# Output projection's weights in eight-row runs per partition, with the attention output reordered on the chip to match

## The chip, the cores and the metric

The kernel runs on one core of one Trainium2 chip. The metric is the device time of one execution in microseconds (us). Three runs of the kernel before gave 369.44, 369.52 and 369.91 us, a median of 369.52 us. The profile was taken on one further execution of 369.39 us.

## The reference, cut to what matters

One decode step of a gated mix of two branches. Branch A is attention over the last 2048 positions of a cache (8 batches, 32 query heads on 16 key/value heads of width 128), followed by an output projection with `wo` (4096 x 576). Branch B is a layer norm and a two-layer network of width 4608 with biases `b1` and `b2`. A gate per batch mixes them.

```python
g = sigmoid((A_x * gate_w).sum(-1, keepdims=True))
q = (A_x @ wq)                                   # 8 x 32 heads x 128
p = softmax(q . k[last 2048] * 128 ** -0.5)
a = (p @ v[last 2048]).reshape(8, 1, 4096) @ wo  # 4096 x 576
b = gelu(layernorm(B_x) @ w1 + b1) @ w2 + b2     # 576 -> 4608 -> 576
out = g * a + (1 - g) * b                        # 8 x 1 x 576
```

Nearly all of the data is the cache: 32 units of keys and 32 of values, each of 2 MB.

## The kernel before

**The plan.** The kernel isn't written in the order in which it runs. Every piece of work is an `_Op` with an engine, a cost estimate, dependencies (`deps`, for which the engine waits) and order-only predecessors (`after`). `_Plan.schedule` plays the program through with those estimates and so fixes the list of each engine; `emit` then writes the lists out, each op with its waits on the semaphores of its `deps`. At run time each engine goes through its own list from the top, so an op that waits holds everything behind it in that list. Where an op stands in the list is thus decided by estimated times and not by the real ones. For transfers the estimate has two forms, and the size that is passed to `dma(...)` chooses between them:

```python
if op.nbytes < 65536:
    op.t1 = est + 0.4 + self.DMA_LAT            # DMA_LAT = 1.8
else:
    start = max(est + 0.4, dma_free)            # behind all earlier large transfers
    dma_free = start + op.nbytes / self.DMA_BW
    op.t1 = dma_free + self.DMA_LAT
```

**The transfers.** All large loads are issued by SP, in the order of the list `stream` (from L540): five units of keys (K0 to K4), then a K unit and a V unit in turn, a chunk of `wo` (W0 to W3) after every eighth V unit, then the bias `b2` ("B") and four chunks of `w2` (M0 to M3). Its end reads ... V23, W2, K29, V24, K30, V25, K31, V26, V27, V28, V29, V30, V31, W3, B, M0, M1, M2, M3. The loads go round nine slots of 2 MB in SBUF; each waits until its slot is free. By that rule W3 waits for the transposes of K30, M0 for the value matmuls of V25, M1 for the transposes of K31, M2 for the value matmuls of V26 and M3 for those of V27; V31 waits for those of V24, V30 for the transposes of K29 and V29 for the projection with W2. `b2` has a place of its own and waits for nothing but its turn in SP's list.

**Keys** (`k_unit`, L612 on). A K unit is one of four quarters of a group of two key heads; there are eight groups. DVE transposes its two halves (L630, "tr"), with two buffers for the results, and PE multiplies each half with the queries (L644, "qk", eight matmuls a half). After the fourth quarter comes the softmax of the group (`softmax`, L574 on): maximum on DVE (L577), small steps (L580 to L586), four exponentials on ACT (L591), four transposes on DVE (L596), the sum over the positions (L599, L600, one PE matmul at L601, a reciprocal at L602), and at L606 `rg`, the reciprocal times the gate.

**Values** (`v_unit`, L656 on). PE multiplies the probabilities with a V unit (L667, "pv", sixteen matmuls), ACT copies the result out of PSUM (L673, "ovac"), PE sums and transposes it (L678, "osel"). After two V units, one "item" (a key head with two query heads and all eight batches) is complete: ACT copies it (L689, "oev"), and POOL multiplies it with `rg` into `oT` (L697). The last item, 15, does without ACT and POOL: there DVE reads PSUM directly. `oT` holds, for each of the 32 heads, the 128 head columns on the partitions and the eight batches beside each other.

**Projection and second layer.** `wo_chunk` (L701 on) loads eight heads' rows of `wo`, so that partition p gets row p of each head: eight runs of 1152 bytes a partition. `AccGroup` (L523 to L536) adds products into one PSUM bank: for each pair (left operand, right operand) two matmuls of 288 columns (L532), one per half of the 576 output columns. Four such groups belong to a W chunk, one per item. `bias` (L716 on) loads `b2` onto eight partitions in one transfer (L717) and adds it in with a group "m2_b" of four matmuls; `m2_chunk` (L721 on, transfers at L728) does the same for `w2`, the last chunk in three pieces. At the end DVE and ACT copy half of the bank each (L746, L747), and two transfers write the output (L749).

**PE's list around the end of the value stream**, before the change: qk of K30, pv of V25, osel of V25, qk of K31, pv of V26, osel of V26, pv of V27, the sum of the last group (L601), osel of V27, then pv and osel of V28 to V31 in turn, and last 92 matmuls of L532: 16 for the four items of W3, 4 of "m2_b", 72 of `w2`.

Of the kernel before, what the change touches and what calls it, by code (L numbers as in the profile page):

```python
# [171 lines left out]
def build_kernel(nc, A_x, A_k_cache, A_v_cache, A_wq, A_wo, B_x, B_w1, B_b1, B_w2, B_b2, gate_w, out):  # L172
# [24 lines left out]
    with ExitStack() as es:  # L197
# [39 lines left out]
        req("sm", 32 * NG, F32)  # L237
        req("dsum", 32, F32)
        req("rr", 32, F32)
        req("rg", 2 * 32, F32)  # L240
        req("o32", 2 * 16, F32)
        req("oT", Hkv * 16, BF)
        req("out_sb", JN, BF)
        req("PT", 2 * 2048, BF)
        req("P", 2048, BF)
# [57 lines left out]
        rg = view("rg").rearrange("p (g m) -> p g m", g=2)  # L303
        o32 = view("o32").rearrange("p (u m) -> p u m", u=2)
        oT = view("oT").rearrange("p (u h b) -> p u h b", u=Hkv, h=2)
# [20 lines left out]
        def col(i, parts=128):  # L326
# [9 lines left out]
        BK_ACC = 7  # L336

        eng_sems = {e: es.enter_context(nc.semaphore("sem_" + e)) for e in ENGS}
        dma_keys = ["x", "b", "b2", "wq", "w1", "out", "outb"] + ["s%d" % i for i in range(NSLOT)] + ["t%d" % i for i in range(4)]
        dma_sems = {k: es.enter_context(nc.semaphore("dma_" + k)) for k in dma_keys}  # L340

        P = _Plan()
# [5 lines left out]
        o_ident = add("pool", lambda e: e.affine_select(out=ident, in_=ones_bf[:, 0:128], pattern=[[-1, 128]], compare_op=ALU.is_equal,  # L348
                                                        fill=0.0, base=0, channel_multiplier=1), deps=[o_ones], name="ident", cost=0.3)
        o_idf = add("pool", lambda e: e.tensor_copy(idf8, ident[0:8, 0:8]), deps=[o_ident], name="idf8", cost=0.15)  # L350
        o_nhalf = add("pool", lambda e: e.memset(col(C_NHALF, 8), -0.5), name="nhalf", cost=0.1)
        o_xz0 = add("pool", lambda e: e.memset(view("xz", 8), 0.0), name="xz0", cost=0.2)
        o_yz0 = add("pool", lambda e: e.memset(view("yz", 8), 0.0), name="yz0", cost=0.2)
# [207 lines left out]
        o_ev, o_sel = {}, {}  # L561
        proj_ops = {}
        oT_done = {}

        def src_of(cache, g, q):
            hkv, b0 = 2 * g + q // 2, 4 * (q % 2)
# [7 lines left out]
        def softmax(g):  # L574
            k = lambda i, n=1, parts=128, p0=0: sm[p0:p0 + parts, g, i:i + n]
            MX, GA, GB_, GC_, M01, M23, TT, NB, SUM, S = 0, 1, 2, 3, 4, 5, 6, 7, 8, 12
            mx = add("dve", lambda e: e.tensor_reduce(out=k(MX), in_=ps[:, 0:4, :].rearrange("p a n -> p (a n)"), axis=AXL.X, op=ALU.max), deps=[qk_unit[4 * g + 3]], name="mx%d" % g, cost=2.25, prio=5)  # L577
# [22 lines left out]
            ds = add("dve", lambda e: e.tensor_scalar(out=dsum, in0=i32, scalar1=k(S), scalar2=None, op0=ALU.mult), deps=[s_] + o_i32 + ([rg_done[g - 1]] if g else []), name="ds_%d" % g, cost=0.16, prio=5)  # L600
            sp_ = add("pe", lambda e: e.matmul(ps[:, BK_S, 0:32], ones_f, dsum, start=True, stop=True), deps=[ds, o_yT, o_gb], name="sum_pe%d" % g, cost=0.5, prio=5)  # L601
            rc = add("dve", lambda e: e.reciprocal(out=rr, in_=ps[:, BK_S, 0:32]), deps=[sp_], name="rc_%d" % g, cost=0.16, prio=5)  # L602

            def rg_fn(e):
                in1 = bass.AP(arena_f, offset=foffs("gb"), ap=[[AST // 2, 128], [0, 2], [1, 8], [0, 2]])
# [4 lines left out]
            rg_done[g] = add("dve", rg_fn, deps=deps, name="rg_%d" % g, cost=0.16, prio=5)  # L610

        def k_unit(i):  # L612
            g, q = divmod(i, 4)
# [42 lines left out]
        def v_unit(i):  # L656
# [28 lines left out]
            if q % 2 == 1:  # L685
                hl = q // 2
                o_acc = ps[:, BK_OS[0]:BK_OS[1] + 1, 0:8]
                if item < Hkv - 1:
                    ev = add("act", lambda e: e.activation(out=o32[:, item % 2, :].rearrange("p (a n) -> p a n", a=2), in_=o_acc, func=ACTF.Copy), deps=[o_sel[i - 1], o_sel[i]] + ([oT_done[item - 2]] if item >= 2 else []), name="oev%d" % item, cost=0.25, prio=3)  # L689
                    o_item_ev[item] = ev  # L690
                    eng, src_, deps = "pool", o32[:, item % 2, :], [ev, rg_done[g]]
                else:
                    eng, src_, deps = "dve", o_acc, [o_sel[i - 1], o_sel[i], rg_done[g]]

                def om_fn(e):
                    src4 = src_.rearrange("p a (b h) -> p a b h", h=2) if item == Hkv - 1 else src_.rearrange("p (a b h) -> p a b h", a=2, h=2)
                    return e.tensor_tensor(out=oT[:, item, :, :].rearrange("p h (a b) -> p a b h", a=2), in0=src4,  # L697
                                           in1=rg[:, g % 2, 16 * hl:16 * hl + 16].rearrange("p (a b h) -> p a b h", a=2, h=2), op=ALU.mult)
                oT_done[item] = add(eng, om_fn, deps=deps, name="oT%d" % item, cost=0.25, prio=9)

        def wo_chunk(i):  # L701
            s = take_slot()
            h0 = WO_CH * i
            dst = slot(s)[:, 0:WO_CH * WOP].rearrange("p (t c) -> p t c", t=WO_CH)
            d = dma("sp", lambda e: e.dma_start(dst[:, :, 0:D], A_wo[128 * h0:128 * (h0 + WO_CH), :].rearrange("(t p) c -> p t c", p=128)),
                    "s%d" % s, WO_CH * 128 * D * 2, deps=slot_free[s], name="d_wo%d" % i, after=last_dma[-1:])
            last_dma.append(d)
            ops = []
# [3 lines left out]
            slot_free[s] = ops  # L712

        o_m2 = []

        def bias(i):  # L716
            d = dma("sp", lambda e: e.dma_start(b2_sb, B_b2.partition_broadcast(8)), "b2", 65536, name="d_b2", after=last_dma[-1:])  # L717
            last_dma.append(d)
# [101 lines left out]
```

## Time and profile before

| what | value |
|---|---|
| profiled execution, device time | 369.39 us |
| its span, first to last instruction | 367.7 us |
| around the span | 1.7 us |
| PE busy | 260.6 us (71%) |
| DVE busy | 210.0 us (57%) |
| ACT busy | 47.7 us (13%) |
| POOL busy | 37.5 us (10%) |
| read from HBM | 154.31 MB, 420 GB/s over the span |
| mean granted TensorE clock | 0.838 |

"Busy" is the share of the span in which an engine works on an instruction; a wait isn't busy. The start of the span is time 0 in everything that follows. A row of the timeline gives start, duration, engine, line of the kernel, operation, operands, shape and number of instructions merged into the row, and in brackets how long the engine had been idle before it and what ended that. "SPq" rows are the issuing of a transfer by SP, not the transfer; the rows on issues give the time from issue to landing. The rows of DMA packets count packets "under 512 B", "under 2 KB" and "under 8 KB" cumulatively.

### The profile page before, as it was taken

Reading aid. Unit: us, or ns where it says so; the run is one execution under the profiler, and the core shown is the slowest. Engines: PE = TensorE matmul, PEld = TensorE weight load, DVE = VectorE, ACT = ScalarE, POOL = GpSimd, SP = SyncE. Lnnn points to the kernel's source line nnn. Section 1 sums busy time; section 2 is a strip of 40 time slices with the busy share of each in tenths; the row PEclk is TensorE's granted clock in tenths of the full one; section 3 lists DMA queues with packets and bytes.
Section 4 is the critical chain, followed back from the end, with each engine's and each line's share of the span. In section 5 each row is a group of like instructions: output and inputs, shape, how many; then the busy total and the mean of one; then the engine's idle time right before and its main releaser. Section 6 shows DMA issues by size and latency. Waiting matters only on the chain.

```text
span 367.7 us, 4525 instructions
## 1 busy us (share of the span) xinstructions
PE 260.6 (71%) x1815; PEld 130.1 (35%) x1837; DVE 210.0 (57%) x253; ACT 47.7 (13%) x117; POOL 37.5 (10%) x163
## 2 busy tenths in 40 slices
PE   0259983897596779774978496784976496874897
PEld 0159430353342234332433242232432242332453
DVE  0704699797694474459744844469644864473000
ACT  1010002100300121003000300003000300004100
POOL 7011010011021002000101010010110000000000
PEclk9999998799698869887879878887898789795558
DMA  8999999999999999999999999999999999999995
GB/s 345 428 414 431 428 430 431 430 428 431 426 430 431 419 433 433 428 428 429 431 430 428 414 439 429 430 430 431 431 430 430 419 430 430 433 430 431 409 426 206
DMA packets 14924, 154.60 MB, mean 420 GB/s; under 512 B 1292, under 2 KB 5428, under 8 KB 6072
## 3 DMA queue, kind: packets, MB, share of 16 engines
q1 hardware_dynamic: 14848, 154.29, 98.9%
q8 instruction: 14, 0.23, 0.2%
q14 instruction: 6, 0.05, 0.0%
q10 hardware_dynamic: 56, 0.03, 0.0%
HBM read 154.31 MB, written 0.01 MB: 420 GB/s over the span
## 4 chain that ended last, share of the span: by engine, by line
DMA 62%; PE 17%; DVE 16%; SPq 3%; issue 1%; ACT 1%; DVEq 0%; ACTq 0%
DMA arena<-in_A_k_cache_dram 50%; DMA arena<-in_B_w_dram 11%; DVE arena L630 11%; PE ps L644 9%; DVE arena L577 2%; PE ps L489 2%; PE ps L667 2%; PE ps L678 1%; SPq L728 1%; SPq L660 1%; PE ps L640 1%; DVE arena L596 1%; PE ps L491 1%; DVE arena L580 0%; DVE arena L586 0%
## 5 line engine op out<-in xcount | busy, mean ns | idle before, releaser
L630 DVE STREAM_TRANSPOSE arena<-arena 128x2048 f32<-128x2048 f32 x64 | 145.2, 2296 | 73.8 <-DMA arena<-in_A_k_cache_dram 72.1
L644 PE MATMUL ps<-arena 128*128 128x512 bf16 x496 | 147.3, 449 | 27.2 <-DVE arena L630 25.8
L644 PEld LDWEIGHTS ps<-arena 128*128 128x128 bf16 x512 | 53.1, 111 | 112.8 <-issue 39.4
L623 POOL COPY arena<-arena 32x32 bf16<-32x32 bf16 x128 | 26.0, 203 | 216.9 <-PE ps L644 202.3
L678 PE MATMUL ps<-arena 128*128 128x8 f32 x256 | 37.1, 272 | 15.4 <-ACT arena L673 15.4
L678 PEld LDWEIGHTS ps<-arena 128*128 128x128 f32 x256 | 35.7, 212 | 29.3 <-ACT arena L673 28.0
L673 ACT ACTIVATE arena<-ps 128x512 f32<-128x512 f32 x32 | 19.1, 598 | 197.9 <-PE ps L667 197.9
L667 PE MATMUL ps<-arena 128*32 128x512 bf16 x512 | 37.0, 413 | 3.0 <-DMA arena<-in_A_v_cache_dram 2.3
L640 PE MATMUL ps<-arena 128*128 128x512 bf16 x26 | 12.6, 629 | 34.5 <-DVE arena L596 30.5
L577 DVE TENSOR_REDUCE arena<-ps 128x1 f32<-128x2048 f32 x8 | 18.2, 2281 | 17.9 <-PE ps L644 17.9
L591 ACT ACTIVATE arena<-ps,arena 128x512 bf16<-128x512 f32 x32 | 21.5, 685 | 41.1 <-DVE arena L586 41.1
L596 DVE STREAM_TRANSPOSE arena<-arena 128x512 bf16<-128x512 bf16 x32 | 19.9, 674 | 0.9 <-ACT arena L591 0.9
L667 PEld LDWEIGHTS ps<-arena 128*32 128x32 bf16 x512 | 11.3, 100 | 21.2 <-issue 12.4
L640 PEld LDWEIGHTS ps<-arena 128*128 128x128 bf16 x32 | 3.5, 128 | 38.1 <-DVE arena L596 33.6
L489 PE MATMUL ps<-arena 128*128 128x8 bf16 x144 | 10.9, 201 | 3.6 <-DMA arena<-in_B_w_dram 3.6
L532 PE MATMUL ps<-arena 128*8 128x288 bf16 (+1 forms) x140 | 12.9, 344 | 0.4 <-DMA arena<-in_B_w_dram 0.4
L697 POOL TENSOR_TENSOR arena<-arena 128x16 bf16<-128x16 f32 x15 | 4.0, 265 | 83.6 <-ACT arena L689 82.8
L489 PEld LDWEIGHTS ps<-arena 128*128 128x128 bf16 x144 | 10.8, 159 | 4.0 <-DMA arena<-in_B_w_dram 4.0
L697 DVE TENSOR_TENSOR arena<-ps,arena 128x16 bf16<-128x16 f32 x1 | 0.2, 228 | 19.6 <-PE ps L678 19.6
L411 PE MATMUL ps<-arena 8*128 8x8 bf16 x8 | 0.5, 168 | 14.7 <-DVE arena L384 11.0
L602 DVE RECIPROCAL arena<-ps 128x32 f32<-128x32 f32 x8 | 2.9, 357 | 12.4 <-PE ps L601 12.4
L532 PEld LDWEIGHTS ps<-arena 128*8 128x8 bf16 (+1 forms) x140 | 6.3, 99 | 5.8 <-DMA arena<-in_B_w_dram 1.0
(82 smaller groups left out, 91.1 us busy)
## 6 DMA issues: line engine op xcount, KB each, us to landing
arena<-in_A_k_cache_dram SPq DMA_DIRECT2D x32, 2048.0 KB, 34.1
arena<-in_A_v_cache_dram SPq DMA_DIRECT2D x32, 2048.0 KB, 34.3
arena<-in_B_w_dram SPq DMA_DIRECT2D x1, 4608.0 KB, 24.3
arena<-in_A_wo_dram SPq DMA_DIRECT2D x4, 1152.0 KB, 36.8
arena<-in_A_wq_dram SPq DMA_DIRECT2D x1, 4096.0 KB, 12.9
arena<-in_B_w_dram SPq DMA_DIRECT2D x3, 1296.0 KB, 14.8
arena<-in_B_w_dram SPq DMA_DIRECT2D x2, 576.0 KB, 20.6
arena<-in_A_wq_dram SPq DMA_DIRECT2D x1, 512.0 KB, 3.5
```

The costliest lines, as they stand in the source:

```text
L489: ins = e.matmul(out_, lhsT, yT[:, kt, :], start=(kt == 0), stop=False)
L532: ins = e.matmul(ps[32 * j:32 * j + 8, BK_ACC, 0:JN], lhsT, rhs[:, JN * j:JN * j + JN], start=False, stop=True, skip_group_check=True, til ...
L577: mx = add("dve", lambda e: e.tensor_reduce(out=k(MX), in_=ps[:, 0:4, :].rearrange("p a n -> p (a n)"), axis=AXL.X, op=ALU.max), deps=[qk_ ...
L591: return e.activation(out=Pm[:, 512 * c:512 * c + 512], in_=ps[:, c, :], func=ACTF.Exp, bias=k(NB), scale=SCALE, accum_out=k(SUM + c))
L596: pts.append(add("dve", (lambda c=c: lambda e: e.transpose(bass.AP(arena, offset=aoffs("PT") + (g % 2) * 2048 + 128 * c, ap=[[AST, 128], [ ...
L623: return e.tensor_copy(dst, src)
L630: tr = add("dve", (lambda h=h, kb=kb: lambda e: e.transpose(bass.AP(arena_f, offset=foffs("KT") + kb * 2048, ap=[[AST // 2, 128], [1, 2048]]),
L640: mm = e.matmul(ps[:, rc, :], maskL, maskR, start=True, stop=False)
L644: mm = e.matmul(ps[:, rc, :], qbd[:, ub, 2 * h + ee, :], rhs, start=False, stop=(q == 3 and h == 1 and ee == 1))
L667: mm = e.matmul(ps[32 * t:32 * t + 32, BK_OS[i % 2], :], PT[:, g % 2, q, 32 * r4:32 * r4 + 32], slot(s)[:, 512 * r4:512 * r4 + 512], start ...
L673: o_ev[i] = add("act", lambda e: e.activation(out=osb[:, i % 2, :], in_=ps[:, BK_OS[i % 2], :], func=ACTF.Copy), deps=[prev] + ([o_sel[i - ...
L678: mm = e.matmul(ps[:, BK_OS[i % 2], 0:8], osb[:, i % 2, 128 * r:128 * r + 128], i32[:, 8 * r:8 * r + 8], start=(r == 0), stop=(r == 3), sk ...
```

## The change

A chunk of `wo` (1024 rows) is now loaded with eight consecutive rows a partition, one run of 9216 bytes instead of eight of 1152. Partition p then holds rows 8p to 8p+7 of the chunk, that is, column 8(p mod 16)+t of head p div 16 for t = 0 to 7. The attention output has to stand on the partitions in that order too. It is brought there in three steps:

- `rg` becomes eight times as wide (256 instead of 32 elements): it holds reciprocal and gate times a mask `mskt`, which is 1 where the partition number mod 8 is t. POOL's product for an item (`om_fn`) writes, per head, eight masked copies of the eight batches: 128 elements a partition instead of 16. The last item takes the way over ACT and POOL as well.
- Eight matmuls a chunk ("orow", 128 x 128 weights cut from the band matrix `wide`, 64 columns) add up the eight heads so that head h's column 8i+t lands on partition 16h+i, at column group t. They use columns 64 to 127 of the PSUM bank of the softmax sum.
- ACT copies the 64 columns to SBUF ("oPev"), and then one `AccGroup` of eight pairs, sixteen matmuls as before, multiplies them with the chunk. It can start only when all four items of the chunk are complete.

`mskt`, `gbm` (mask times gate) and `wide` are made once at the start. The transfer of `b2` is split into one of six and one of two partitions, each entered in the plan with 32768 bytes instead of one with 65536.

PE's list, as it is built from the changed plan, has these differences. Each of the first three chunks has its eight "orow" matmuls ahead of its sixteen projection matmuls, at the place where the latter stood. At the end stand 8 "orow" matmuls and 88 of the projection and `w2`. The four matmuls of "m2_b" stand between the pv of V25 and the osel of V25, with a wait for both `b2` transfers. In SP's list `b2` stands where it stood, behind W3.

```diff
+        o_wd0 = add("pool", lambda e: e.affine_select(out=wide, in_=ones_bf[:, 0:240], pattern=[[-8, 240]], ...
+        o_wide = add("pool", lambda e: e.affine_select(out=wide, in_=wide, pattern=[[8, 240]], ...
+        o_mskt = add("dve", lambda e: e.tensor_reduce(out=mskt, in_=ident.rearrange("p (k t) -> p t k", t=WO_CH), axis=AXL.X, op=ALU.add),
+        o_gbm = add("dve", gbm_fn, deps=[o_mskt, o_gb], name="gbm", cost=0.25, prio=-1)
...
-                return e.tensor_tensor(out=rg[:, g % 2, :].rearrange("p (l b h) -> p l b h", l=2, b=8), in0=rr.rearrange("p (l b h) -> p l b h", l=2, b=8), in1=in1, op=ALU.mult)
-            deps = [rc, o_gb]
+                in0 = bass.AP(arena_f, offset=foffs("rr"), ap=[[AST // 2, 128], [0, WO_CH], [16, 2], [1, 16]])
+                in1 = bass.AP(arena_f, offset=foffs("gbm"), ap=[[AST // 2, 128], [16, WO_CH], [0, 2], [1, 16]])
+                return e.tensor_tensor(out=rg[:, g % 2, :, :].rearrange("p t (l n) -> p t l n", l=2), in0=in0, in1=in1, op=ALU.mult)
+            deps = [rc, o_gbm]
...
-                if item < Hkv - 1:
-                    ev = add("act", ... name="oev%d" % item, cost=0.25, prio=3)
-                    eng, src_, deps = "pool", o32[:, item % 2, :], [ev, rg_done[g]]
-                else:
-                    eng, src_, deps = "dve", o_acc, [o_sel[i - 1], o_sel[i], rg_done[g]]
+                ev = add("act", ... name="oev%d" % item, cost=0.25, prio=3)
+                eng, deps = "pool", [ev, rg_done[g]]
...
+                    out_ = oX[:, (item // WO_IT) % 2, 2 * (item % WO_IT):2 * (item % WO_IT) + 2, :].rearrange("p h (t b) -> p h t b", t=WO_CH)
+                    return e.tensor_tensor(out=out_, in0=in0, in1=in1, op=ALU.mult)
...
-            dst = slot(s)[:, 0:WO_CH * WOP].rearrange("p (t c) -> p t c", t=WO_CH)
-            d = dma("sp", lambda e: e.dma_start(dst[:, :, 0:D], A_wo[128 * h0:128 * (h0 + WO_CH), :].rearrange("(t p) c -> p t c", p=128)),
+            dst = slot(s)[:, 0:WO_CH * D]
+            d = dma("sp", lambda e: e.dma_start(dst, A_wo[128 * h0:128 * (h0 + WO_CH), :].rearrange("(p t) c -> p (t c)", t=WO_CH)),
...
-            for item in range(h0 // 2, (h0 + WO_CH) // 2):
-                mms = [(oT[:, item, h, :], dst[:, 2 * item + h - h0, 0:D]) for h in range(2)]
-                ops.append(AccGroup("proj%d" % item, mms, [oT_done[item], d], cost=0.5).op)
+            def rows_fn(e):
+                for h in range(WO_CH):
+                    mm = e.matmul(ps[:, bk, 64:64 + 8 * WO_CH], wide[:, 112 - 16 * h:240 - 16 * h], oX[:, i % 2, h, :], start=(h == 0), stop=(h == WO_CH - 1), skip_group_check=True)
+                return mm
+            sel_done.append(add("pe", rows_fn, deps=[oT_done[it] for it in its] + [o_wide, rc_last[-1]] + oP_ev[-1:], name="orow%d" % i, cost=0.6))
+            oP_ev.append(add("act", lambda e: e.activation(out=oP[:, i % 2, :], in_=ps[:, bk, 64:64 + 8 * WO_CH], func=ACTF.Copy),
+                             deps=[sel_done[-1]] + ([proj_ops[i - 2]] if i >= 2 else []), name="oPev%d" % i, cost=0.25, prio=3))
+            mms = [(oP[:, i % 2, 8 * t:8 * t + 8], dst[:, t * D:(t + 1) * D]) for t in range(WO_CH)]
+            proj_ops[i] = AccGroup("proj%d" % i, mms, [oP_ev[-1], d], cost=0.25 * WO_CH).op
...
-            d = dma("sp", lambda e: e.dma_start(b2_sb, B_b2.partition_broadcast(8)), "b2", 65536, name="d_b2", after=last_dma[-1:])
-            o_m2.append(AccGroup("m2_b", [(ob[:, 0:8], b2_sb), (ob[:, 8:16], b2_sb)], [d, o_obl, o_obh], cost=0.6).op)
+            for r0, r1 in ((0, 6), (6, 8)):
+                d = dma("sp", (lambda r0=r0, r1=r1: lambda e: e.dma_start(b2_sb[r0:r1, :], B_b2.partition_broadcast(r1 - r0)))(), "b2%d" % r0, 32768, name="d_b2_%d" % r0, after=last_dma[-1:])
+            o_m2.append(AccGroup("m2_b", [(ob[:, 0:8], b2_sb), (ob[:, 8:16], b2_sb)], ds + [o_obl, o_obh], cost=0.6).op)
```

More of the change, by code (lines that the diff above doesn't have):

```diff
@@ L191, in build_kernel @@
     WO_CH = 8
+    WO_IT = WO_CH // 2
     JN = D // NJ
@@ L239, in build_kernel @@
         req("rr", 32, F32)
-        req("rg", 2 * 32, F32)
+        req("rg", 2 * WO_CH * 32, F32)
+        req("gbm", WO_CH * 16, F32)
+        req("mskt", WO_CH, F32)
+        req("wide", 128 + 112, BF)
+        req("oX", 2 * WO_CH * WO_CH * 8, BF)
+        req("oP", 2 * WO_CH * 8, BF)
         req("o32", 2 * 16, F32)
-        req("oT", Hkv * 16, BF)
         req("out_sb", JN, BF)
@@ L302, in build_kernel @@
         rr = view("rr")
-        rg = view("rg").rearrange("p (g m) -> p g m", g=2)
+        rg = view("rg").rearrange("p (g t m) -> p g t m", g=2, t=WO_CH)
+        mskt, wide = view("mskt"), view("wide")
+        oX = view("oX").rearrange("p (g h n) -> p g h n", g=2, h=WO_CH)
+        oP = view("oP").rearrange("p (g n) -> p g n", g=2)
         o32 = view("o32").rearrange("p (u m) -> p u m", u=2)
-        oT = view("oT").rearrange("p (u h b) -> p u h b", u=Hkv, h=2)
         out_sb = view("out_sb")
@@ L338, in build_kernel @@
         eng_sems = {e: es.enter_context(nc.semaphore("sem_" + e)) for e in ENGS}
-        dma_keys = ["x", "b", "b2", "wq", "w1", "out", "outb"] + ["s%d" % i for i in range(NSLOT)] + ["t%d" % i for i in range(4)]
+        dma_keys = ["x", "b", "b20", "b26", "wq", "w1", "out", "outb"] + ["s%d" % i for i in range(NSLOT)] + ["t%d" % i for i in range(4)]
         dma_sems = {k: es.enter_context(nc.semaphore("dma_" + k)) for k in dma_keys}
@@ L350, in build_kernel @@
         o_idf = add("pool", lambda e: e.tensor_copy(idf8, ident[0:8, 0:8]), deps=[o_ident], name="idf8", cost=0.15)
+        o_wd0 = add("pool", lambda e: e.affine_select(out=wide, in_=ones_bf[:, 0:240], pattern=[[-8, 240]], compare_op=ALU.is_ge,
+                                                      fill=0.0, base=896, channel_multiplier=1), deps=[o_ones], name="wide0", cost=0.4, prio=-1)
+        o_wide = add("pool", lambda e: e.affine_select(out=wide, in_=wide, pattern=[[8, 240]], compare_op=ALU.is_ge,
+                                                       fill=0.0, base=-889, channel_multiplier=-1), deps=[o_wd0], name="wide1", cost=0.4, prio=-1)
         o_nhalf = add("pool", lambda e: e.memset(col(C_NHALF, 8), -0.5), name="nhalf", cost=0.1)
@@ L447, in build_kernel, with gbm_fn @@
                              deps=[o_ident, o_obl], name="i32_%d" % q, cost=0.15, prio=-1))
+        o_mskt = add("dve", lambda e: e.tensor_reduce(out=mskt, in_=ident.rearrange("p (k t) -> p t k", t=WO_CH), axis=AXL.X, op=ALU.add),
+                     deps=[o_ident, o_obl], name="mskt", cost=0.25, prio=-1)
+        def gbm_fn(e):
+            a0 = bass.AP(arena_f, offset=foffs("mskt"), ap=[[AST // 2, 128], [1, WO_CH], [0, 8], [0, 2]])
+            a1 = bass.AP(arena_f, offset=foffs("gb"), ap=[[AST // 2, 128], [0, WO_CH], [1, 8], [0, 2]])
+            return e.tensor_tensor(out=view("gbm").rearrange("p (t b h) -> p t b h", b=8, h=2), in0=a0, in1=a1, op=ALU.mult)
+        o_gbm = add("dve", gbm_fn, deps=[o_mskt, o_gb], name="gbm", cost=0.25, prio=-1)
         def q_fn(e):
@@ L600, in softmax @@
             ds = add("dve", lambda e: e.tensor_scalar(out=dsum, in0=i32, scalar1=k(S), scalar2=None, op0=ALU.mult), deps=[s_] + o_i32 + ([rg_done[g - 1]] if g else []), name="ds_%d" % g, cost=0.16, prio=5)
[L601 removed]
+            sp_ = add("pe", lambda e: e.matmul(ps[:, BK_S, 0:32], ones_f, dsum, start=True, stop=True), deps=[ds, o_yT, o_gb] + oP_ev[-1:], name="sum_pe%d" % g, cost=0.5, prio=5)
             rc = add("dve", lambda e: e.reciprocal(out=rr, in_=ps[:, BK_S, 0:32]), deps=[sp_], name="rc_%d" % g, cost=0.16, prio=5)
+            rc_last.append(rc)
             def rg_fn(e):
[L605 to L607 removed]
+                in0 = bass.AP(arena_f, offset=foffs("rr"), ap=[[AST // 2, 128], [0, WO_CH], [16, 2], [1, 16]])
+                in1 = bass.AP(arena_f, offset=foffs("gbm"), ap=[[AST // 2, 128], [16, WO_CH], [0, 2], [1, 16]])
+                return e.tensor_tensor(out=rg[:, g % 2, :, :].rearrange("p t (l n) -> p t l n", l=2), in0=in0, in1=in1, op=ALU.mult)
+            deps = [rc, o_gbm]
             if g >= 2:
                 deps.append(oT_done[2 * (g - 2) + 1])
[L610 removed]
+            rg_done[g] = add("dve", rg_fn, deps=deps, name="rg_%d" % g, cost=0.35, prio=5)
         def k_unit(i):
@@ L687, in v_unit @@
                 o_acc = ps[:, BK_OS[0]:BK_OS[1] + 1, 0:8]
-                if item < Hkv - 1:
-                    ev = add("act", lambda e: e.activation(out=o32[:, item % 2, :].rearrange("p (a n) -> p a n", a=2), in_=o_acc, func=ACTF.Copy), deps=[o_sel[i - 1], o_sel[i]] + ([oT_done[item - 2]] if item >= 2 else []), name="oev%d" % item, cost=0.25, prio=3)
-                    o_item_ev[item] = ev
-                    eng, src_, deps = "pool", o32[:, item % 2, :], [ev, rg_done[g]]
-                else:
-                    eng, src_, deps = "dve", o_acc, [o_sel[i - 1], o_sel[i], rg_done[g]]
-                def om_fn(e):
[L696 to L699, printed above, removed]
+                ev = add("act", lambda e: e.activation(out=o32[:, item % 2, :].rearrange("p (a n) -> p a n", a=2), in_=o_acc, func=ACTF.Copy), deps=[o_sel[i - 1], o_sel[i]] + ([oT_done[item - 2]] if item >= 2 else []), name="oev%d" % item, cost=0.25, prio=3)
+                o_item_ev[item] = ev
+                eng, deps = "pool", [ev, rg_done[g]]
+                def om_fn(e):
+                    in1 = bass.AP(arena_f, offset=foffs("rg") + (g % 2) * WO_CH * 32 + 16 * hl, ap=[[AST // 2, 128], [1, 2], [32, WO_CH], [2, 8]])
+                    in0 = bass.AP(arena_f, offset=foffs("o32") + 16 * (item % 2), ap=[[AST // 2, 128], [1, 2], [0, WO_CH], [2, 8]])
+                    out_ = oX[:, (item // WO_IT) % 2, 2 * (item % WO_IT):2 * (item % WO_IT) + 2, :].rearrange("p h (t b) -> p h t b", t=WO_CH)
+                    return e.tensor_tensor(out=out_, in0=in0, in1=in1, op=ALU.mult)
+                oT_done[item] = add(eng, om_fn, deps=deps, name="oT%d" % item, cost=0.45, prio=9)
         def wo_chunk(i):
@@ new lines, in wo_chunk @@
+            its = range(h0 // 2, (h0 + WO_CH) // 2)
+            sel_done.append(add("pe", rows_fn, deps=[oT_done[it] for it in its] + [o_wide, rc_last[-1]] + oP_ev[-1:], name="orow%d" % i, cost=0.6))
+            oP_ev.append(add("act", lambda e: e.activation(out=oP[:, i % 2, :], in_=ps[:, bk, 64:64 + 8 * WO_CH], func=ACTF.Copy),
+                             deps=[sel_done[-1]] + ([proj_ops[i - 2]] if i >= 2 else []), name="oPev%d" % i, cost=0.25, prio=3))
+            mms = [(oP[:, i % 2, 8 * t:8 * t + 8], dst[:, t * D:(t + 1) * D]) for t in range(WO_CH)]
```

10 lines of the change are left out of this document (7 added, 3 removed).

## The prediction

> **What bounds the kernel now.** I read the page first: how full the transfers are.
>
> ```profile
> DMA  8999999999999999999999999999999999999995
> q1 hardware_dynamic: 14848, 154.29, 98.9%
> arena<-in_A_v_cache_dram SPq DMA_DIRECT2D x32, 2048.0 KB, 34.3
> ```
>
> The DMA engines are full in every slice but the first and the last, 98.9% over the span, and a V unit lands 34.3 us after its issue: about seven units of 4.9 us (2.1 MB at 430 GB/s) are queued ahead of it. The kernel is bound by its transfers until they end. How the end hangs on them is in the chain of waits from 290 us on:
>
> ```profile
> 291.49 28.71 DMA arena<-in_A_k_cache_dram
> 320.22 4.52 DVE arena L630 x2
> 324.78 1.99 PE ps L644 x8
> 326.79 2.30 DVE arena L577
> ...
> 337.50 1.92 PE ps L667 x16
> ...
> 364.86 0.43 PE ps L532 x4
> ```
>
> The last key unit, K31, lands at 320.2. From there a serial stretch leads to the end: transposes, qk, the last softmax (maximum at 326.79, first pv after it at 337.50), four times pv and osel, projection and `w2`. PE's timeline shows this stretch, with the speeds that I need:
>
> ```profile
> 312.91 4.45 PE L644 MATMUL ps<-arena 128*128 128x512 bf16 x10 [2.63 <-DVE arena L630]
> 317.58 1.31 PE L644 MATMUL ps<-arena 128*128 128x512 bf16 x5 [0.23 <-issue]
> 318.83 1.05 PE L667 MATMUL ps<-arena 128*32 128x512 bf16 x16
> 320.58 1.06 PE L678 MATMUL ps<-arena 128*128 128x8 f32 x8 [0.70 <-ACT arena L673]
> ...
> 324.78 1.97 PE L644 MATMUL ps<-arena 128*128 128x512 bf16 x8 [0.21 <-DVE arena L630]
> ...
> 334.83 0.64 PE L601 MATMUL ps<-arena 128*128 128x32 f32 x2 [3.82 <-DVE arena L600]
> ...
> 353.74 1.88 PE L678 MATMUL ps<-arena 128*128 128x8 f32 x8 [0.70 <-ACT arena L673]
> 355.54 8.43 PE L532 MATMUL ps<-arena 128*8 128x288 bf16 x82
> 364.15 0.53 PE L532 MATMUL ps<-arena 128*8 128x288 bf16 x6 [0.19 <-DMA arena<-in_B_w_dram]
> 364.86 0.41 PE L532 MATMUL ps<-arena 128*8 128x288 bf16 x4 [0.17 <-DMA arena<-in_B_w_dram]
> ```
>
> PE works from 355.54 to the end and waits for the last `w2` pieces only 0.19 and 0.17 us. So PE's stretch from K31 and the transfers arrive together at 365; shortening one alone gains little, and a delay of PE's stretch is paid in full. PE also has two speeds: at 312.91 ten matmuls take 0.43 us each, at 317.58 five take 0.25. Two windows show the clock granted to it, the third figure from the end of a row: 1.00 up to 331, then 0.52, after PE had rested 3.82 us ahead of the row at 334.83.
>
> ```profile
> 326.00:331.00 5.00, 3.83 (x44) 1.74 (x42) 3.67 (x11) 0.67 (x2) 0.00 (x0) 1.00 1.00 426
> 331.00:337.00 6.00, 2.18 (x12) 2.17 (x10) 3.55 (x8) 3.20 (x9) 0.00 (x0) 0.52 1.01 434
> ```
>
> **The transfer that moves, and when it lands.** The change puts "m2_b" on PE's list between the pv of V25 (the row at 318.83) and its osel (the row at 320.58). Before, it stood among the last 92 matmuls. The plan takes any transfer under 65536 bytes to land 2.2 us after issue; each half of `b2` is now entered with 32768, so the plan thinks that it is there. But it is issued behind W3 on a queue that is 34 us deep. SP's issues, and the packets in the time after:
>
> ```profile
> 315.12 0.37 SPq L705 DMA_DIRECT2D arena<-in_A_wo_dram  x1
> 315.54 0.52 SPq L717 DMA_DIRECT2D arena<-in_B_b_dram  x1
> 319.92 26.37 SPq L728 DMA_DIRECT2D arena<-in_B_w_dram  x1
> ...
> DMA packets 895, 13.08 MB, mean 430 GB/s; under 512 B 96, under 2 KB 96, under 8 KB 96
> ...
> arena<-in_B_w_dram SPq DMA_DIRECT2D x1, 1296.0 KB, 35.5
> ...
> DMA packets 1172, 2.42 MB, mean 396 GB/s; under 512 B 40, under 2 KB 1072, under 8 KB 1072
> ```
>
> The first packet row is the stretch 315.6 to 346.0, just after `b2` was issued: 96 packets under 2 KB, and the same 96 under 512 B, so not one row of 1152 bytes passed, and a row of `b2` has 1152 bytes. The second is 346.0 to 352.1: 1072 less 40 is 1032, the 1024 rows of W3 and the 8 of `b2`. So `b2` travels with W3, 30 us and more after its issue. M0, next in the queue, lands at 319.92 + 35.5 = 355.4; less its 1.33 MB at 430 GB/s (3.1 us) the queue had passed `b2` at 352.3. I take that as its landing before the change.
>
> SP needs nothing from behind the stalled matmuls: V31 waits for the pv of V24, W3 for the transposes of K30, M0 for the pv of V25, M1 for the transposes of K31 (they need the qk of K30), all ahead of "m2_b". So it is a stall that ends and no lock. M2 and M3 wait for the pv of V26 and V27 and are issued only after the stall.
>
> **The `wo` transfers.** Four windows around the chunks, and one stretch without:
>
> ```profile
> 118.00:127.00 9.00, 7.96 (x39) 3.19 (x38) 4.62 (x7) 0.60 (x1) 0.81 (x4) 0.72 1.01 431
> 127.00:133.00 6.00, 1.97 (x5) 0.74 (x6) 5.70 (x14) 2.78 (x8) 0.00 (x0) 0.74 1.04 407
> 208.60:214.60 6.00, 4.37 (x11) 1.74 (x13) 5.41 (x8) 1.11 (x4) 0.00 (x0) 0.50 1.05 406
> 289.40:295.50 6.10, 2.25 (x6) 1.01 (x8) 5.97 (x11) 2.78 (x8) 0.00 (x0) 0.58 1.05 411
> 346.00:352.00 6.00, 4.94 (x38) 2.92 (x42) 0.00 (x0) 0.78 (x2) 0.27 (x1) 0.50 1.02 394
> ```
>
> The last two figures are DMA share and GB/s. Without a chunk it is 431 GB/s, with one 407, 406, 411 and 394. The same bytes at 431 would have saved 6.00 x (1 - 407/431) = 0.33, and 0.35, 0.28 and 0.52 us: 1.5 us in all. Bounds: nothing, if the long runs of 9216 bytes go no faster; twice as much, 3.0 us, if packets overlap more than the rates show. I take 1.5. `b2` lands behind all four chunks, so it comes 1.5 us earlier: 352.3 - 1.5 = **350.8**.
>
> The Trainium skill (DMA: Bandwidth & Descriptors, Specifications) puts the shortest transfer for line rate at 512 B; by that, rows of 1152 bytes would already run at full rate and the sum would be 1.5 us longer. The four windows, 394 to 411 against 431 GB/s, speak against it.
>
> **The stall.** PE reaches "m2_b" when the pv of V25 ends, 318.83 + 1.05 = 319.9 (about 1 us earlier with faster chunks), and waits until 350.8: 32 us. Behind it on PE's list stands all that is left: osel 25, qk of K31, pv 26 and on. DVE can finish K31's two transposes meanwhile (two buffers); then it, ACT and POOL wait for PE. Nothing covers this: the old stretch from 320.6 to 365.3 now begins at 350.8.
>
> Its pieces, PE at the slow speed at first after so long a rest:
>
> - "m2_b", 4 matmuls at 0.10 (row of L532 below): to 351.2. Osel 25 at 1.88 instead of 1.06: to 353.1.
> - qk of K31, 16 matmuls, both halves ready. Slow for the first 4.7 us after the rest, as at 312.91 to 317.58: five or six at 0.43 until 355.5, the other ten or eleven at 0.25: to 358.2. Before, that point was 326.79, so the delay is 31.4 us. All at 0.25 would be 0.9 less, all at 0.43 1.8 more.
> - The last softmax, pv and osel 28 to 31: as before, 326.79 to 353.74 + 1.88 = 355.62; now to **387.0**. Pv 26 and 27 fit beside the maximum, and PE then rests over 4 us (3.82 before), so the stretch runs slowly as before.
>
> **The longer way of the last item.** Prices from the groups of instructions:
>
> ```profile
> L697 POOL TENSOR_TENSOR arena<-arena 128x16 bf16<-128x16 f32 x15 | 4.0, 265 | 83.6 <-ACT arena L689 82.8 <-POOL arena L623 0.2
> L363 POOL COPY arena<-arena 128x128 bf16<-128x128 bf16 x4 | 1.0, 282 | 0.0
> L355 POOL TENSOR_SCALAR_AFFINE_SELECT arena<-arena 128x512 bf16<-128x512 bf16 x1 | 1.6, 1550 | 0.0
> L689 ACT ACTIVATE arena<-ps 128x16 f32<-128x16 f32 x15 | 2.7, 183 | 29.7 <-PE ps L678 29.7
> L489 PE MATMUL ps<-arena 128*128 128x8 bf16 x144 | 10.9, 201 | 3.6 <-DMA arena<-in_B_w_dram 3.6
> L532 PE MATMUL ps<-arena 128*8 128x288 bf16 (+1 forms) x92 | 9.4, 374 | 0.4 <-DMA arena<-in_B_w_dram 0.4
> ```
>
> Before, DVE's product of item 15 lay beside the first matmuls of the tail (PE did not pause after 355.54). Now there follow in series: oev 15 on ACT 0.2; POOL's product with 128 elements for 16, between 0.28 (a copy of that size, 282 ns) and 2.1 (eight times 265), taken as 0.8, nearer the copy; eight "orow" matmuls between 0.6 (144 of L489 in 10.9 us, 0.08 each) and 1.6 (201 ns each), taken as 1.0; "oPev" on ACT at 0.22, little over oev; four handovers of 0.07. Sum 2.5 us, bounds 1.6 and 4.4. To 389.5. Then 88 matmuls at 9.4/92 = 0.102: 9.0 us, to **398.5**. M2 and M3, issued at about 359 and 362, need some 3 us each and are long there. From PE's last matmul (365.27) to the end of the span were 2.4 us: 400.9. With the 1.7 around the span: **402.6 us**, 33.2 over the profiled 369.39, which stands 0.13 under the median of the runs.
>
> **Costs set to nothing.** The first twelve items on POOL and "orow"/"oPev" of three chunks lengthen PE's way at those places by about the same 2.5 us each; eight times a wider `rg`, and `mskt` and `gbm` once, are small products on DVE; `wide` is two selects on POOL at the start, at most 1.55 us each (row of L355, which has twice the elements). The transfers hide all of that:
>
> ```profile
> L630 DVE STREAM_TRANSPOSE arena<-arena 128x2048 f32<-128x2048 f32 x64 | 145.2, 2296 | 73.8 <-DMA arena<-in_A_k_cache_dram 72.1 <-PE ps L644 1.2
> L395 POOL TENSOR_TENSOR arena<-arena 8x1 f32<-8x1 f32 x1 | 0.6, 563 | 8.4 <-DVE arena L394 8.4
> ```
>
> DVE waits 72.1 us for keys and POOL 8.4 us at the start. Without that cover the three chunks alone would cost 7.5 us; the queue of 34 us is a second cover.
>
> **The rivals.**
>
> 1. `b2` lands early, as the plan thinks, and PE does not stall. For it: the transfers are two small ones on few partitions. Against it: no packet of its size in 30 us of the old profile. It decides at the point where `b2` lands before about 319, when PE gets there. Then the end is the old one: 365.27, less 1.0 for three chunks ahead of K31, plus 2.5 for item 15, less 0.4 for four matmuls moved forward and 0.36 of waits filled: 366.0, or 370.1 us; with item 15 at its lower bound 369.2. I give it 369.6: no change, within the 0.2% that a measurement of this kernel can tell.
> 2. The stall comes, but PE is fast in the tail. For it: the granted clock was 1.00 just before the last softmax. Against it: it was 0.50 after a rest of 3.82 us, and that rest stays. It would save 4 x 0.87 on pv (1.92 against 1.05) and 5 x 0.82 on osel, 7.6 us, and by the same ratio up to 4 us on the last 88 matmuls; with half of that, 393 us.
> 3. The layout brings no gain in the queue, or PE stays slow through the qk of K31: 404 to 405 us.
>
> **How the numbers follow.** Forecast with rival 3 inside its range 0.86; rival 2 0.06; rival 1 0.08. Predicted 402.6. Downward 1.5 (chunks) and 0.9 (qk) and 0.9 (item 15), upward 1.5, 1.8 and 1.9, not all at once: 399 to 406.5; reaching a little toward rival 2, 398 to 406.5. The other cases hold less than 2 in 10 outside. Slower 0.86 + 0.06 + 0.02 of rival 1: 0.94; the same 0.04; faster 0.02.
>
> **What would show it.** Right: PE idle some 32 us from 319 on, ended by the transfer of `b2`; the maximum of the last group near 358; DMA empty from about 357 until M2; no slow windows at the chunks. Wrong: "m2_b" done near 320 without idle time, or a tail with granted clock 1.00, or a gap of DMA at a `wo` chunk earlier on.

## The result, and the profile after

The changed kernel takes 401.9 us (median of 5 runs, 401.41 to 402.57) against 369.52 us: a ratio of 1.0876 with a 95% interval of 1.086 to 1.0892, slower by 32.4 us. The prediction was 402.6 us. The profiled execution took 401.79 us, with a span of 400.0.

First the page of the changed kernel: transfers over the 40 slices of its span.

```profile
DMA  8999999999999999999999999999999999956000
GB/s 356 413 428 426 424 435 425 436 428 428 433 429 423 437 428 433 433 430 433 428 424 434 433 425 433 429 433 431 433 429 430 426 436 429 428 236 265 2 0 3
q1 hardware_dynamic: 11264, 154.29, 90.6%
```

The transfers are as full as before up to slice 35 (350 us), and the last three slices are empty: the data has long arrived and the kernel still works. There are 3584 packets fewer (11264 for 14848), which are the 4096 short rows of `wo` less the 512 long ones. PE's timeline of the changed kernel shows where the 33 us went:

```profile
316.26 1.05 PE L690 MATMUL ps<-arena 128*32 128x512 bf16 x16
351.19 0.64 PE L552 MATMUL ps<-arena 8*8 8x288 bf16 x4 [33.88 <-DMA arena<-in_B_b_dram]
351.76 1.88 PE L701 MATMUL ps<-arena 128*128 128x8 f32 x8
353.49 6.45 PE L667 MATMUL ps<-arena 128*128 128x512 bf16 x16
...
368.01 0.64 PE L622 MATMUL ps<-arena 128*128 128x32 f32 x2 [4.36 <-DVE arena L621]
...
386.92 1.88 PE L701 MATMUL ps<-arena 128*128 128x8 f32 x8 [0.70 <-ACT arena L696]
389.85 0.58 PE L734 MATMUL ps<-arena 128*128 128x64 bf16 x8 [1.06 <-POOL arena L719]
390.75 6.81 PE L552 MATMUL ps<-arena 128*8 128x288 bf16 x88 [0.31 <-ACT arena L738]
```

The second row is "m2_b": four matmuls ahead of which PE stood still for 33.88 us, ended by the transfer of `b2`. The pv of V25 is the row above it, osel 25 and the qk of K31 the rows below, in the order of the new list. Then everything comes that before lay between 320 and 365. The chain of waits of the changed kernel goes through the same place:

```profile
314.63 36.52 DMA arena<-in_B_b_dram
351.15 0.04 issue
351.19 0.64 PE ps L552 x4
```

`b2` was issued at 314.63 and landed 36.5 us later, at 351.15. The packets in two stretches, 315 to 348 and 348 to 351.2, answer to those of before:

```profile
DMA packets 1006, 14.19 MB, mean 430 GB/s; under 512 B 111, under 2 KB 111, under 8 KB 111
...
DMA packets 174, 1.38 MB, mean 431 GB/s; under 512 B 27, under 2 KB 35, under 8 KB 35
```

In the first, all 111 packets under 2 KB are under 512 B, so again no row of `b2`, 1152 bytes long, passes in 33 us. In the second there are 8 more, the 8 rows of `b2`. (W3's rows have 9216 bytes now and no longer show here.)

### The profile page after: what moved, and what is told of

Read it like the earlier page. It is cut to its first block, busy times and chain, and to the rows that moved or that the text cites. A ratio compares the mean times of both kernels' runs of the same rounds, so it can differ in the third digit from the quotient of the medians.

```text
span 400.0 us, 4620 instructions
## 1 busy us (share of the span) xinstructions
PE 267.8 (67%) x1869; PEld 132.7 (33%) x1869; DVE 212.0 (53%) x254; ACT 48.8 (12%) x122; POOL 42.3 (11%) x166
## 3 DMA queue, kind: packets, MB, share of 16 engines
q1 hardware_dynamic: 11264, 154.29, 90.6%
## 4 chain that ended last, share of the span: by engine, by line
DMA 62%; PE 19%; DVE 13%; issue 3%; ACT 1%; POOL 0%; SPq 0%; POOLq 0%; DVEq 0%; ACTq 0%
DMA arena<-in_A_k_cache_dram 47%; DMA arena<-in_B_b_dram 9%; DVE arena L653 9%; PE ps L667 8%; DMA arena<-in_B_w_dram 6%; PE ps L509 2%; PE ps L552 2%; PE ps L690 2%; PE ps L701 2%; DVE arena L598 2%; PE ps L663 1%; DVE arena L617 1%; PE ps L511 1%; DVE arena L607 0%; DVE arena L601 0%
## 5 line engine op out<-in xcount | busy, mean ns | idle before, releaser
L667 PE MATMUL ps<-arena 128*128 128x512 bf16 x512 | 152.3, 454 | 16.2 <-DVE arena L653 16.2
L667 PEld LDWEIGHTS ps<-arena 128*128 128x128 bf16 x512 | 54.2, 112 | 105.6 <-issue 43.0
L701 PEld LDWEIGHTS ps<-arena 128*128 128x128 f32 x256 | 36.5, 217 | 28.6 <-ACT arena L696 26.8
L663 PE MATMUL ps<-arena 128*128 128x512 bf16 x32 | 14.9, 621 | 33.2 <-DVE arena L617 28.5
L552 PE MATMUL ps<-arena 128*8 128x288 bf16 (+1 forms) x140 | 11.3, 321 | 35.1 <-DMA arena<-in_B_b_dram 33.9
L719 POOL TENSOR_TENSOR arena<-arena 128x128 bf16<-128x128 f32 x16 | 8.1, 508 | 124.3 <-ACT arena L711 123.5
L663 PEld LDWEIGHTS ps<-arena 128*128 128x128 bf16 x32 | 3.5, 128 | 38.9 <-DVE arena L617 34.5
L509 PEld LDWEIGHTS ps<-arena 128*128 128x128 bf16 x144 | 10.8, 159 | 4.6 <-DMA arena<-in_B_w_dram 4.6
L711 ACT ACTIVATE arena<-ps 128x16 f32<-128x16 f32 x16 | 2.9, 183 | 66.6 <-PE ps L701 66.6
```

Source lines behind the costliest of these rows:

```text
L509: ins = e.matmul(out_, lhsT, yT[:, kt, :], start=(kt == 0), stop=False)
L552: ins = e.matmul(ps[32 * j:32 * j + 8, BK_ACC, 0:JN], lhsT, rhs[:, JN * j:JN * j + JN], start=False, stop=True, skip_group_check=True, til ...
L663: mm = e.matmul(ps[:, rc, :], maskL, maskR, start=True, stop=False)
L667: mm = e.matmul(ps[:, rc, :], qbd[:, ub, 2 * h + ee, :], rhs, start=False, stop=(q == 3 and h == 1 and ee == 1))
L701: mm = e.matmul(ps[:, BK_OS[i % 2], 0:8], osb[:, i % 2, 128 * r:128 * r + 128], i32[:, 8 * r:8 * r + 8], start=(r == 0), stop=(r == 3), sk ...
```

## The experiments

Two theories were to be told apart. Theory 1, that of the prediction: the whole loss is PE's wait at "m2_b", for a transfer that the plan takes for landed while it stands behind 34 us of loads; the new layout by itself nearly breaks even. Theory 2: the reordering (masked copies, selection matmuls, copies out of PSUM) costs what is lost. A third question is why `b2` is late: for its place in SP's queue, or because the DMA engines are full for anyone.

**Undo the plan's mistake alone.**

```diff
-                d = dma("sp", ..., "b2%d" % r0, 32768, name="d_b2_%d" % r0, after=last_dma[-1:])
+                d = dma("sp", ..., "b2%d" % r0, 65536, name="d_b2_%d" % r0, after=last_dma[-1:])
```

> The changed kernel, but the two halves of b2 are entered in the plan with 65536 bytes each, so that m2_b comes behind osel of V31 on PE's list; layout, transfers and everything else stay. Theory 1 (PE's stall at m2_b is the whole loss): the stall of 32 us goes, and what is left is the layout's gain of 1.0 us ahead of K31 against about 2.0 us of the last item's longer way: 369.7 us (369.0 to 370.5). Theory 2 (the masked copies, selection matmuls and copies out of PSUM are what costs): it stays near 400 us.

Measured: 369.71 us, ratio to the kernel before 1.0008 (0.9999 to 1.0017). One number that only the plan reads, and no instruction but the place of four matmuls, gives back 32 us. PE's timeline of this run, end:

```profile
354.85 1.88 PE L701 MATMUL ps<-arena 128*128 128x8 f32 x8 [0.70 <-ACT arena L696]
356.66 0.64 PE L552 MATMUL ps<-arena 8*8 8x288 bf16 x4
357.78 0.59 PE L734 MATMUL ps<-arena 128*128 128x64 bf16 x8 [0.48 <-POOL arena L719]
358.68 6.66 PE L552 MATMUL ps<-arena 128*8 128x288 bf16 x88 [0.31 <-ACT arena L738]
```

"m2_b" stands behind the last osel, with no idle time. From the last osel (356.73) to the first of the 88 matmuls PE spends 1.95 us on item 15's longer way; "m2_b" lies within it.

**The mistake alone, in the old kernel.**

```diff
-            d = dma("sp", lambda e: e.dma_start(b2_sb, B_b2.partition_broadcast(8)), "b2", 65536, ...)
+            for r0, r1 in ((0, 6), (6, 8)):
+                d = dma("sp", ..., "b2%d" % r0, 32768, name="d_b2_%d" % r0, after=last_dma[-1:])
```

> The kernel before, with only b2 split into six and two partitions and each half entered with 32768 bytes, so that m2_b stands between pv and osel of V25; old layout of wo, no reordering. Theory 1: the stall alone gives nearly the whole loss. b2 lands some 1.3 us later than in the changed kernel, the last item saves its 2 us: about 401 us (399.5 to 402.5). Theory 2: 369.5 to 370.5.

Measured: 400.55 us, 1.084 (1.0824 to 1.0857). PE's timeline of this run:

```profile
318.93 1.05 PE L667 MATMUL ps<-arena 128*32 128x512 bf16 x16
352.52 0.64 PE L532 MATMUL ps<-arena 8*8 8x288 bf16 x4 [32.54 <-DMA arena<-in_B_b_dram]
```

The old kernel with nothing but the split and its two numbers loses 31 us: theory 1 holds from both sides, and theory 2 falls.

**The same place, another queue.** "m2_b" is held between the pv and the osel of V25, and ACT issues `b2` when that pv is done.

```diff
-                d = dma("sp", ..., after=last_dma[-1:])
-                last_dma.append(d)
-                ds.append(d)
+                ds.append(dma("act", ..., deps=[pv_hist[25]], name="d_b2_%d" % r0))
+            grp = AccGroup("m2_b", ..., after=[pv_hist[25]])
...
+            o_sel[25].after.append(grp.op)
```

> The changed kernel with m2_b at its place between pv and osel of V25, but both halves of b2 issued by ACT on its own queue when the pv of V25 is done, about the time at which SP issued them. Theory 1 in full (what delays b2 is its place behind the loads on SP's queue): it lands 2 to 5 us after its issue, most of the stall goes: 371 to 374 us. Rival (any transfer waits that long because all DMA engines are full): stall of some 30 us as before, 400 to 403 us.

Measured: 371.97 us, 1.0059 (1.0029 to 1.0088). ACT's issue and PE's wait in this run:

```profile
317.31 0.59 ACTq L749 DMA_DIRECT2D arena<-in_B_b_dram x2
...
322.93 0.64 PE L552 MATMUL ps<-arena 8*8 8x288 bf16 x4 [5.68 <-DMA arena<-in_B_b_dram]
```

The same 9 KB, issued 2.7 us later on DMA engines that are as full (436 GB/s from 317 to 323), arrive 5.6 us after their issue and not 36.5. So it is the place behind the loads on SP's queue that delays `b2`, and not the load on the engines. The 5.6 us is one sample: the ten executions of this kernel lie between 369.42 and 374.45 us, a wider spread than that of any other here, and only one of them has a trace.

**The layout without the reordering.**

```diff
-            dst = slot(s)[:, 0:WO_CH * WOP].rearrange("p (t c) -> p t c", t=WO_CH)
-            d = dma("sp", lambda e: e.dma_start(dst[:, :, 0:D], A_wo[...].rearrange("(t p) c -> p t c", p=128)),
+            dst = slot(s)[:, 0:WO_CH * D].rearrange("p (t c) -> p t c", t=WO_CH)
+            d = dma("sp", lambda e: e.dma_start(slot(s)[:, 0:WO_CH * D], A_wo[...].rearrange("(p t) c -> p (t c)", t=WO_CH)),
```

> The kernel before, with only the transfers of wo in runs of 9216 bytes; attention output not reordered, so the projection multiplies rows that do not belong together: it leaves the reordering out. Both theories: the price of the layout's transfers alone, K31 1.0 us earlier and the last transfers 1.5 us earlier: 368.3 us (367.8 to 369.0). If long runs are no faster: 369.5. The difference to e1_b2_size is the price of the reordering: theory 1 up to 2 us, theory 2 30 us.

Measured: 368.44 us, 0.9973 (0.9964 to 0.9982). The long rows alone save 1.05 us. Four windows of this run at the chunks, the last figure in GB/s:

```profile
127.00:133.00 6.00, 2.73 (x7) 1.01 (x8) 5.90 (x10) 2.78 (x8) 0.00 (x0) 0.66 1.00 426
209.00:215.00 6.00, 2.70 (x7) 1.15 (x9) 5.96 (x8) 2.78 (x8) 0.00 (x0) 0.66 1.02 431
291.00:297.00 6.00, 2.72 (x7) 1.18 (x9) 5.96 (x8) 2.75 (x8) 0.00 (x0) 0.65 1.01 431
346.00:352.00 6.00, 5.13 (x40) 2.76 (x40) 0.00 (x0) 0.62 (x2) 0.27 (x1) 0.50 1.01 423
```

With the short rows the prediction read 407, 406, 411 and 394. The Trainium skill (DMA: Bandwidth & Descriptors, Specifications), by whose 512 B rows of 1152 bytes would already go at line rate, has this run against it. Beside e1_b2_size (both against 369.49 us) the kernel with the reordering takes 1.27 us more, which is more than the layout brings. That is not the price of the added work alone. The qk of K31 and the last matmuls, first in e1_b2_size, then in this run:

```profile
321.67 6.20 PE L667 MATMUL ps<-arena 128*128 128x512 bf16 x16 [2.77 <-DVE arena L653]
```

```profile
322.02 1.97 PE L644 MATMUL ps<-arena 128*128 128x512 bf16 x8 [1.56 <-DVE arena L630]
324.22 1.97 PE L644 MATMUL ps<-arena 128*128 128x512 bf16 x8 [0.22 <-DVE arena L630]
...
354.98 8.84 PE L532 MATMUL ps<-arena 128*8 128x288 bf16 x88
363.99 0.41 PE L532 MATMUL ps<-arena 128*8 128x288 bf16 x4 [0.17 <-DMA arena<-in_B_w_dram]
```

Between the two profiled executions, 0.95 us apart, three differences add up. In e1_b2_size PE runs this qk at a granted clock of 0.50 up to 326 and ends it 1.7 us later, although K31 landed no later (319.29 against 319.65). Item 15's longer way adds 2.0 us. The last matmuls take 6.66 us instead of 9.42 and give 2.8 us back: the clock rises at about 361 in both, but in e1_b2_size more of them come after that, and there are four fewer. Whether the reordering or chance made PE rest and slow down ahead of K31 wasn't tried.

**Where the reordering costs: the last chunk in the old way**, the rest as in e1_b2_size.

```diff
+            if i == 3:
+                d = dma("sp", lambda e: e.dma_start(dst3[:, :, 0:D], A_wo[...].rearrange("(t p) c -> p t c", p=128)), ...)
...
+                for item in range(h0 // 2, (h0 + WO_CH) // 2):
+                    mms = [(oT[:, item - Hkv + 4, h, :], dst3[:, 2 * item + h - h0, 0:D]) for h in range(2)]
```

> As e1_b2_size, but the last chunk W3 and its items 12 to 15 keep the old layout and the old way (item 15 on DVE straight out of PSUM). Theory 1: the gain of the three chunks ahead of K31 remains, 1.0 us, and the longer way of item 15 is gone: 368.4 us (368.0 to 368.9). Theory 2: the three other chunks' selection matmuls still cost, so it is no faster than 369.5.

Measured: 368.76 us, 0.9983 (0.9974 to 0.9992). With the chunk that nothing covers in the old way, three chunks in the new one are a gain of 0.7 us: their reordering costs less than their rows bring, and nearly all of it lies under the transfers (e4_layout_only, with no reordering at all, is 0.3 us faster).

**`b2` first.** In both of these it comes at the start on ACT's queue:

```diff
-            for r0, r1 in ((0, 6), (6, 8)): ...
+            d = dma("act", lambda e: e.dma_start(b2_sb, B_b2.partition_broadcast(8)), "b20", 8 * D * 2, name="d_b2", after=[d_b1])
```

> As e3_last_chunk_old, and b2 is loaded in one transfer at the start, on ACT's queue ahead of the large loads, so that m2_b stands at the start of PE's list. Theory 1: m2_b waits for nothing long and leaves the tail; 368.4 less up to 0.4 for four matmuls: 368.2 us (367.7 to 368.8). Theory 2: as e3_last_chunk_old.

> The changed kernel in full, with b2 loaded in one transfer at the start on ACT's queue, m2_b at the start of PE's list. Theory 1: no stall, 369.3 to 370.2 us, as e1_b2_size. Theory 2: near 400 us.

Measured: 368.72 us, 0.998 (0.9971 to 0.9989), with the last chunk in the old way, and 370.0 us, 1.0011 (1.0002 to 1.002), with the full new layout. The first is no faster than e3_last_chunk_old (368.76): the 0.4 us of four matmuls that I expected from it did not come, because its end is set by the transfers, as PE's timeline shows:

```profile
363.55 0.53 PE L556 MATMUL ps<-arena 128*8 128x288 bf16 x6 [0.40 <-DMA arena<-in_B_w_dram]
364.25 0.41 PE L556 MATMUL ps<-arena 128*8 128x288 bf16 x4 [0.17 <-DMA arena<-in_B_w_dram]
```

**An earlier start of PE's last stretch**, in e7_b2_first and, as a control, in the kernel before.

```diff
+        stream.remove(("K", NUQ - 1))
+        stream.insert(stream.index(("V", 25)), ("K", NUQ - 1))
```

> As e7_b2_first (full new layout, b2 first), and the load of K31 stands ahead of that of V25 instead of behind it, so PE's last stretch can start 4.9 us earlier. If PE's stretch from K31 with the longer way of item 15 is what ate the layout's gain, the end is now set by the last w2 piece, as in e4_layout_only: 368.3 us (367.9 to 368.8), 1.0 to 1.7 under e7_b2_first. If the gain of the layout went elsewhere: 369.5 to 370.

> Control: the kernel before with K31 ahead of V25 and nothing else. The end stays with the last w2 piece, which the old layout does not bring earlier: 369.2 us (368.9 to 369.6). If the order of the loads alone were the gain of e8_k31_earlier, it would be 368.3 here too.

Measured: 368.64 us, 0.9979 (0.997 to 0.9987), and 369.6 us, 1.0002 (0.9994 to 1.0011) for the control. Both times lie in the ranges expected, the control at the upper edge of its own: the order of the loads alone gains nothing. The reason that I gave for the first did not hold. Rows of e7_b2_first, then of e8_k31_earlier (the matmul of the last softmax sum, the eight of "orow", the last 88):

```profile
335.19 0.64 PE L622 MATMUL ps<-arena 128*128 128x32 f32 x2 [4.36 <-DVE arena L621]
...
357.04 0.58 PE L734 MATMUL ps<-arena 128*128 128x64 bf16 x8 [1.06 <-POOL arena L719]
357.93 8.04 PE L552 MATMUL ps<-arena 128*8 128x288 bf16 x88 [0.31 <-ACT arena L738]
```

```profile
330.12 0.63 PE L624 MATMUL ps<-arena 128*128 128x32 f32 x2 [4.12 <-DVE arena L623]
...
356.37 0.59 PE L736 MATMUL ps<-arena 128*128 128x64 bf16 x8 [1.06 <-POOL arena L721]
357.26 7.09 PE L552 MATMUL ps<-arena 128*8 128x288 bf16 x88 [0.31 <-ACT arena L740]
```

The sum comes 5.1 us earlier, the 88 matmuls only 0.7: one more pv and osel, 4.4 us, now stand behind the sum, because K31 passed V25. PE still works to the end without waiting for `w2`, so PE sets the end and not the last piece. Of the 1.6 us between the two profiled executions, 0.7 is the earlier start and 0.95 the shorter run of 88 matmuls, and that follows the granted clock (third figure from the end), again e7_b2_first ahead of e8_k31_earlier:

```profile
360.00:363.00 3.00, 3.00 (x30) 1.68 (x26) 0.00 (x0) 0.00 (x0) 0.00 (x0) 0.50 0.67 270
```

```profile
360.00:362.00 2.00, 2.00 (x34) 1.33 (x30) 0.00 (x0) 0.00 (x0) 0.00 (x0) 0.89 0.73 294
```

At 0.50 PE does 30 matmuls in 3 us, at 0.89 it does 34 in 2. Whether the edit or chance moved that moment wasn't tried. Like e6_best this kernel is 0.2% faster than the kernel before, and the two can't be told apart.

## Why the prediction was right

The mechanism, its place and its size came as forecast; the time is 0.7 us off. By the steps:

- **`b2` lands at 350.8**: it was 351.15. The queue passes it as worked out; the chunks' gain up to that point was 1.2 us (352.3 before) and not 1.5. Against e2_stall_only, which has the old rows and reaches "m2_b" at 352.52, it is 1.3.
- **A stall of 32 us from about 319**: 33.88 us, from 317.31. PE got there 2.6 us earlier than before and not 1; that changed nothing, since the landing of `b2` sets the end of the stall.
- **The qk of K31 done at 358.2**: the maximum of the last group starts at 359.98, 1.8 us later. Of these, 0.35 us come from the landing of `b2`, 0.2 from "m2_b" and osel 25, and 1.2 from the sixteen matmuls, which took 6.3 us where 5.1 were assumed (6.9 if all had been slow). The clock came back later than the 4.7 us that the sum used. This is the largest term missed upward.
- **From the maximum to the last osel as before, 28.8 us**: 359.98 to 388.80, 28.8 us. PE was slow throughout, after a rest of 4.36 us; rival 2 (a fast tail) did not come.
- **Item 15's longer way, 2.5 us**: 388.80 to 390.75, 1.95 us. POOL's product took 0.51 (0.8 assumed), the eight matmuls 0.58 (1.0), ACT's copy 0.22 (0.22).
- **88 matmuls in 9.0 us**: 6.81 us. This is the largest miss downward, 2.2 us. The duration was taken from the 92 of before, most of which ran at a clock of 0.50; here the clock rose on the way:

```profile
391.00:393.00 2.00, 2.00 (x20) 1.14 (x18) 0.00 (x0) 0.00 (x0) 0.00 (x0) 0.50 0.00 0
393.00:395.00 2.00, 2.00 (x34) 1.36 (x30) 0.00 (x0) 0.00 (x0) 0.00 (x0) 0.91 0.00 0
395.00:397.60 2.60, 2.56 (x42) 1.64 (x38) 0.00 (x0) 0.00 (x0) 0.00 (x0) 1.00 0.03 6
```

So two misses of the clock, 1.2 us upward and 2.2 downward, and two smaller ones of 0.55 each way partly cancelled: that 402.6 is only 0.7 us off is in part luck.

- **Rival 1 (no stall, 370.1 us)** did not occur, but its sum can be tested: e1_b2_size and e7_b2_first come close to that kernel, with 369.71 and 370.0 us against the sum's 370.1. In e1_b2_size this too is a sum of parts that cancel (a slower qk, faster last matmuls).
- **The costs set to nothing**: e3_last_chunk_old is faster than the kernel before with three reordered chunks and the wide `rg`, so these lie under the transfers, to within the 0.3 us above.
- **The signs**: the DMA engines ran dry until M2 was issued, as forecast. The window in the changed kernel, with DMA share and GB/s at its end:

```profile
357.50:361.00 3.50, 3.42 (x23) 1.01 (x21) 1.02 (x1) 0.03 (x1) 0.00 (x0) 0.76 0.00 0
```

The slow windows at the chunks are gone as well: 127 to 133, 210 to 216, 291 to 297 and 346 to 352 us have 423, 436, 436 and 424 GB/s in the changed kernel.

## What to carry to other kernels

Where a list is ordered by estimated times, an estimate that is wrong for one small transfer can cost more than all the work of a change: look in the built list for what a moved wait holds up, and in the trace for how long the queue ahead of its transfer is. A small load that is needed late goes ahead of the bulk, or on a queue of its own; issued behind 34 us of loads it takes 36. And a gain in a stream of transfers counts only as far as the engine that ends beside it is shortened too: here 1.05 us of gain met 2.0 us of work behind the last item, in the only chunk that nothing covers, and the clock granted to PE decided what was left of either.

## What the runs showed of the hardware beyond that

**Many short rows hold up the next issue.** Issues of SP in the kernel before and in the changed one (minimum, median and maximum in ns):

```profile
L615 SPq DMA_DIRECT2D arena<-in_A_k_cache_dram x32: 534/548/23619, 2.6 to 291.5; - x32
```

```profile
L638 SPq DMA_DIRECT2D arena<-in_A_k_cache_dram x32: 534/535/1017, 2.6 to 282.3; - x32
```

Behind a chunk of 1024 rows an issue took up to 23.6 us (26.4 for the first `w2` chunk, shown in the prediction); with 128 rows a chunk no K issue takes over 1.0 us, and in e4_layout_only, where nothing but the layout differs, none over 1.2. The DMA engines stayed full meanwhile (98.9% over the span), so no cost shows, but SP could issue nothing else.

**The clock comes back later than assumed.** In the changed kernel PE works without a break from 351.2 on:

```profile
351.20:355.00 3.80, 3.80 (x16) 2.35 (x17) 0.00 (x0) 0.18 (x1) 0.50 (x1) 0.50 0.95 400
355.00:358.00 3.00, 3.00 (x8) 1.01 (x7) 0.00 (x0) 0.00 (x0) 0.00 (x0) 0.50 0.28 114
358.00:360.00 2.00, 2.00 (x10) 0.65 (x12) 0.02 (x1) 0.00 (x0) 0.00 (x0) 0.70 0.00 0
```

The granted clock is 0.50 for at least 6.8 us and rises within the third window; the shorter stretch from 358.5 to 359.0 still has 0.50, which makes it 7.8 us. Before, at 312.91, it took 4.7 us after a rest of 2.63. The Trainium skill (TensorE: Matmul & The Clock Gate, Part 1) gives about 3.4 us of sustained work, in a window that does not start with the work. If a whole window must pass behind the start of the work, that makes 3.4 to 6.8 us, an estimate from the page's figure: the 4.7 us lie within it, the 7.8 us do not. What else delays the clock after a rest of 34 us wasn't tried.
